# Moving one of four exps of 53 attention bursts from ScalarE to VectorE, with the TensorE work around those bursts regrouped

## The chip, the cores and the metric

The kernel runs on one core of a Trainium2 chip. In this kernel TensorE does the matrix products and leaves their sums in PSUM (`f_ps` in the views), which the program divides into eight banks of 512 columns. ScalarE does the exps and VectorE the other elementwise work; in the views both read PSUM and write SBUF, the working memory (`f_pt<-f_ps` and `f_K<-f_ps`). In the views of the profile PE is TensorE, PEld its weight loads, ACT is ScalarE, DVE is VectorE, POOL and SP are two more engines, and a q behind a name is its sequencer. A name such as L1565 is a line of the kernel. Times are microseconds on the device. A time is the median of several runs. A ratio is the mean time of one kernel's fast runs over that of the other's fast runs of the same rounds, so it is not quite the ratio of the medians.

The kernel before takes 961.2 us (960.95 to 961.47, 4 runs).

## The reference, cut to what matters

The reference mixes a state-space layer and an attention layer with a gate. The change touches the attention, which has 2048 tokens, 32 heads of 32 columns, and a full (not causal) softmax:

```python
qkv = (x @ wqkv).reshape(B, S, 3, H, Dh) ...          # S = 2048, H = 32, Dh = 32
scores = jnp.einsum("bhqd,bhkd->bhqk", q, k) * (Dh ** -0.5)
p = _softmax(scores, axis=-1)
o = jnp.einsum("bhqk,bhkd->bhqd", p, v)
...
return g * a + (1 - g) * b                             # a: state-space layer, b: attention @ wo
```

That is 32 x 2048 x 2048 exps. The inputs are small: worked out from the reference's own inputs, the scaled scores have a standard deviation of 0.006 and none exceeds 0.046 in size. So every exp lies within 5% of 1.

## The kernel before

The attention is cut into 512 *bursts*. A burst is 4 heads x 256 queries x 256 keys:

1. TensorE computes the scores (8 matmuls) into two *score slots* of PSUM, of two banks each. There are three such slots.
2. ScalarE computes two exps of 128x1024, one for each slot (two heads each), and writes each into a *tile* of SBUF.
3. Later TensorE multiplies the tile with V: 4 *groups* of 4 small products per burst, summed in one PSUM bank. Eight bursts form a unit, which VectorE normalizes.

The same loop also feeds TensorE with *dense chains* (projections, the state-space layer, the output product): chains of mostly 8 or 16 products of 128x512 into one PSUM bank, which VectorE must evacuate before the next chain can start. Four dense products go into each burst.

The loop, cut, in the order in which it hands work to the engines:

```python
for p in range(first, NBURST):
    self.burst(p)                       # scores of burst p, then its two exps
    q0, q1 = self.quarters[p]
    self.pv(q0, q1)                     # groups of V products planned for this place
    if q1 % 32 == 0:
        self.normalize(q1 // 32 - 1)
    ...                                 # loads (cut)
    quota = MM_PER_PERIOD               # 4
    while used < quota: ...             # dense products (cut)
    ...                                 # VectorE work that fits (cut)
    if ended is not None:
        ended.evac()                    # VectorE empties the dense bank
```

The plan of the V products and the tiles, cut (left out: a rule that allows six groups at a place where 6 to 12 of the unit are left, and the tiles of the first 60 bursts):

```python
n = min(4 * (p - 1), done + 5, done // 32 * 32 + 32)   # a burst's groups: at most 5 a place,
self.quarters[p] = (done, n)                           # not before place B + 2
...
def pt_of(self, B, z):                                 # z = 0, 1: the two exps of a burst
    return self.pt_at[B][z] if B < RING else (2 * B + z) % 6
```

There are six tiles and a burst takes two of them. So a tile is written again by the exps of the burst three later. Dependencies are kept with tokens, in the order of this program: an operation that reads a tile depends on the operation that wrote it last *before it in the program*. In place `p` the exps of burst `p` come first and the V products after them. A V product of burst `B` therefore finds its own exps in the tile only up to place `B + 2`. In the kernel before, every group from burst 60 on stands at exactly that place. (Earlier bursts stand later, but they have more tiles, in memory that is still free then.)

Of the kernel before, what the change touches and what calls it, by code (L numbers as in the profile page):

```python
# [8 lines left out]
I32 = mybir.dt.int32  # L9
ACT = mybir.ActivationFunctionType  # L10
# [13 lines left out]
RC_MAX = 1e20  # L24
# [904 lines left out]
MM_PER_PERIOD = 4  # L929
REST = 508  # L930
# [15 lines left out]
class FastPath:  # L946

    def __init__(self, nc, S, es, d, flag):
# [55 lines left out]
        self.tile += [self.cT[ri][:, j, :].rearrange("p (h n) -> p h n", h=2) for j in range(8) for ri in range(2)]  # L1004

# [308 lines left out]
    def item_ops(self, j, ch, n):  # L1314
# [29 lines left out]
        hw = ["warm"] if ch == 0 and j == 0 else []  # L1344
        if b == 1 and j == 0:
            hw = ["fX", "fY", "m_c"] + self.EFtok + ["gp%d" % i for i in range(4)]
# [164 lines left out]
    def plan(self):  # L1511


        self.quarters, done = {}, 0
        used = {}
        for p in range(FIRST, NBURST + 1):
            n = min(4 * (p - 1), done + (12 if p < FIRST + 0 else 5), done // 32 * 32 + 32)
            left = done // 32 * 32 + 32 - done
            if 5 < left < 13 and 4 * (p - 1) >= done + 6:
                n = done + 6  # L1520
            self.quarters[p] = (done, n)
            for q in range(done, n):
                used[q // 4] = p
            done = n
        order = [8 * int(w[1]) + int(w[3]) for w in self.OPENING.split() if w[0] == "B"]
        assert sorted(order) == list(range(FIRST))
        when = {b: p for p, b in enumerate(order)}

        pairs = [((12 + t, 16 + t), FIRST + 4 + 14 * t) for t in range(4)] + [((10, 11), FIRST + 6)]
        pairs += [((20 + 2 * j, 21 + 2 * j), C_LOADS + 4 * j) for j in range(8)] + [((6, 7), 68), ((8, 9), 68)]  # L1530
        pairs += [((2 * r, 2 * r + 1), NBURST) for r in range(3)]
        free = {t: -9 for t, _ in pairs}
        self.pt_at = {}
        for b in sorted(range(RING), key=lambda b: when.get(b, b)):
            p = when.get(b, b)
            ok = [(end, t) for t, end in pairs if free[t] < p and used[b] < end and not (end == NBURST and used[b] >= RING + t[0] // 2)]
            assert ok, (b, p)

            near = [(end, t) for end, t in ok if end - used[b] <= 1]
            end, t = min(near) if near else max(ok)  # L1540
            free[t] = used[b]
            self.pt_at[b] = t

    def pt_of(self, B, z):
        return self.pt_at[B][z] if B < RING else (2 * B + z) % 6

    def burst(self, B):
# [15 lines left out]
        for z in range(2):  # L1563
            s, p = sl[z], self.pt_of(B, z)
            self.act(lambda e, s=s, p=p: e.activation(self.tile[p], ps[:, 2 * s:2 * s + 2, :], ACT.Exp, scale=SCALE), [("S", s)], [("pt", p)], "exp")  # L1565

    def pv(self, q0, q1):

        ps, V = self.ps, self.V
        for q in range(q0, q1):  # L1570
            B, z, kl = q // 4, q // 2 % 2, q % 2
            U, i = divmod(B, BURSTS)
            g = U // QUNITS
            p = self.pt_of(B, z)

            def mm(e, z=z, p=p, kl=kl, i=i, g=g):
                m = None
                for h2 in range(2):
                    for qt in range(2):
# [3 lines left out]
                                     start=(i == 0 and z == 0 and kl == 0 and h2 == 0 and qt == 0), stop=(i == BURSTS - 1 and kl == 1),  # L1583
                                     skip_group_check=True)
                return m
            kw = dict(writes=["O"]) if i == 0 and z == 0 and kl == 0 else dict(acc=["O"])
            self.S.op("pe", mm, reads=[("pt", p), ("V", g % 2, i // 2), "v1"], name="pv", **kw)

    def normalize(self, U):
# [10 lines left out]
        if g < 4 and qb == 0:  # L1600
            x = [("pt", 6 + t) for t in range(6)] if g else ["wv0", "wv0g"]
            if g == 3:
                assert self.items_done >= 16
                x += [("ub", k, ri) for k in (2, 3) for ri in range(2)]
        self.dma(lambda e: e.dma_start_transpose(self.OT[:, g, 256 * qb:256 * (qb + 1)].rearrange("p (t q) -> p t q", t=2),
# [4 lines left out]
    def build(self):  # L1610
# [4 lines left out]
        self.later, self.tabled, self.folded = [], [], []  # L1615
        self.bg2 = []
# [43 lines left out]
        self.c_end = 0  # L1660
        log = self.log = []
        for p in range(first, NBURST):
# [4 lines left out]
            t0 = PERIOD * (p - first)  # L1667
            period = PERIOD
            q0, q1 = self.quarters[p]
            self.pv(q0, q1)  # L1670
            if q1 % 32 == 0:
                self.normalize(q1 // 32 - 1)
                self.dve_t = max(self.dve_t, t0 + PE_HEAD) + 0.75
# [30 lines left out]
            quota = MM_PER_PERIOD if p >= FIRST + 0 else 0  # L1704
            ended = None
            while used < quota:
# [38 lines left out]
                elif used >= quota and cur.left <= 1 and quota == MM_PER_PERIOD:  # L1745
                    quota += 1
            log.append((p, ended.tag if ended else (cur.tag if cur else None), used, round(self.dve_t - t0, 2), len(self.bg) + len(self.bg2)))
            limit = t0 + (period - 0.1 if ended is not None else period + PE_HEAD)
            while self.bg or self.bg2:
# [17 lines left out]
        assert not outs and cur is None  # L1767
        self.tail()

    def tail(self):  # L1770
# [4 lines left out]
        dve(lambda e: e.memset(z, 0.0), [], ["z"] + [("ut", 1)])  # L1775
# [16 lines left out]
        self.pv(4 * NBURST - 8, 4 * NBURST - 4)  # L1792
        preload()
        self.pv(4 * NBURST - 4, 4 * NBURST)
# [154 lines left out]
```

## Time and profile before

| view | reading |
|---|---|
| span of the profiled run | 960.1 us |
| ScalarE busy | 944.0 us (98%) |
| TensorE busy | 928.0 us (97%, its ends are modelled) |
| VectorE busy | 513.2 us (53%) |
| granted TensorE clock | 0.996 |

From the page of the kernel before: the busy times (share of the span, instructions), and the chain of work that ended last, by engine.

```profile
PE 928.0 (97%) x15316; PEld 490.1 (51%) x15316; DVE 513.2 (53%) x1097; ACT 944.0 (98%) x1034; POOL 10.1 (1%) x39
...
ACT 96%; SPq 1%; PE 1%; DVE 1%; DMA 1%; issue 0%; DVEq 0%
```

The chain is followed back from the last instruction, at each step to what released it. Two engines look full, but only ScalarE (ACT) is on the chain. Busy times over two stretches of the kernel before (start and end in us, then each engine's busy time and instructions, granted clock, DMA share, GB/s):

```profile
48.00:840.00 792.00, 779.17 (x13079) 413.71 (x13079) 453.99 (x936) 792.00 (x864) 5.30 (x18) 1.00 0.25 55
735.00:933.00 198.00, 192.63 (x3146) 98.19 (x3144) 46.91 (x96) 198.00 (x218) 0.00 (x0) 1.00 0.26 79
```

The fourth engine column is ScalarE: it is busy in all of the 792 us and starts 864 activations, one per 0.917 us, so a burst takes 1.83 us. The third is VectorE, busy for 24% of the last stretch, in which 27 of the 53 bursts of the change lie.

What TensorE does in a burst, from the timeline of the kernel before (start, duration, engine, line, what, how many; in brackets how long the engine stood idle just before, and who ended that):

```profile
850.89 0.40 PE L1559 MATMUL f_ps<-f_Q,f_K 32*128 32x256 bf16 x8 [0.28 <-ACT f_pt L1565]
851.22 0.57 PE L1582 MATMUL f_ps<-f_V,f_pt 128*128 128x33 bf16 x16
851.64 1.02 PE L1476 MATMUL f_ps<-f_wb,f_OT 128*128 128x512 bf16 x4
852.72 0.40 PE L1559 MATMUL f_ps<-f_Q,f_K 32*128 32x256 bf16 x8
```

From start to start the scores take 0.33 us, 16 V products 0.42 us, 4 dense ones about 0.86 us (4 x 0.215). The rest of the burst is a wait for ScalarE. The waits of the kernel before (who, for whom: us in total, times, longest):

```profile
PEld f_ps L1559 <- ACT f_pt L1565: 205.8, 464, 1.0
...
PEld f_ps L1582 <- issue: 105.3, 497, 0.4
```

The scores wait for an exp to free their slot. The V products (L1582) wait for no exp: theirs are always done. ("issue" is time in which the engine waited for nothing that the profile shows.)

### The profile page before, as it was taken

The numbers are of one execution on the slowest core, as the hardware profiler recorded it, in microseconds if no ns is written. First come the engines' busy times: TensorE is split into PE (matmuls) and PEld (weight loads), VectorE is DVE, ScalarE is ACT, GpSimd is POOL, SyncE is SP. The second block draws the span as 40 slices with busy tenths as digits, with TensorE's granted clock in tenths as the row PEclk, the third lists the DMA queues.
The fourth block names the chain that finished last, engine by engine and source line by source line (L and its number), as shares of the span: only waits on it lengthen the run. The fifth ranks groups of instructions, "written<-read, shape, count | busy, mean of one in ns | idle before, by whom it ended". The sixth has DMA issues, their size and how long they took to land.

```text
span 960.1 us, 33364 instructions
## 1 busy us (share of the span) xinstructions
PE 928.0 (97%) x15316; PEld 490.1 (51%) x15316; DVE 513.2 (53%) x1097; ACT 944.0 (98%) x1034; POOL 10.1 (1%) x39
## 2 busy tenths in 40 slices
PE   8899999999999999999999999999999999999996
PEld 4555644564444554555545654544645556444443
DVE  2788888898888427112188711178836112232223
ACT  6999999999999999999999999999999999999996
POOL 2000000000000000000000000000000000000000
PEclk9999999999999999999999999999999999999998
DMA  9558434210133002220023210133101213123312
GB/s 203 96 103 131 77 59 85 60 28 29 49 67 79 17 8 62 58 53 17 18 52 62 59 40 24 43 85 60 40 6 39 84 38 118 51 80 118 106 59 72
DMA packets 157074, 60.88 MB, mean 63 GB/s; under 512 B 145664, under 2 KB 145664, under 8 KB 156928
## 3 DMA queue, kind: packets, MB, share of 16 engines
q1 hardware_dynamic: 154768, 58.16, 27.0%
q8 instruction: 121, 1.98, 0.9%
q10 hardware_dynamic: 2160, 0.53, 0.3%
q14 instruction: 25, 0.20, 0.1%
HBM read 16.79 MB, written 12.58 MB: 31 GB/s over the span
## 4 chain that ended last, share of the span: by engine, by line
ACT 96%; SPq 1%; PE 1%; DVE 1%; DMA 1%; issue 0%; DVEq 0%
ACT f_pt L1565 89%; ACT f_OT L1565 2%; ACT f_Et L1565 2%; ACT f_cT_re L1565 2%; ACT f_cT_im L1565 2%; SPq L1040 1%; DMA f_xT<-in_A_x_dram 1%; PE f_ps L1559 0%; PE f_ps L1789 0%; PE f_ps L1582 0%; PE f_ps L1161 0%; PE f_ps L1416 0%; DVE f_xT L1828 0%; PE f_ps L1121 0%; PE f_ps L1815 0%
## 5 line engine op out<-in xcount | busy, mean ns | idle before, releaser
L1565 ACT ACTIVATE f_pt<-f_ps 128x1024 bf16<-128x1024 f32 x944 | 867.1, 1309 | 0.6 <-PE f_ps L1559 0.6
L1582 PEld LDWEIGHTS f_ps<-f_V,f_pt 128*128 128x128 bf16 x7552 | 220.2, 96 | 99.2 <-issue 98.8
L1582 PE MATMUL f_ps<-f_V,f_pt 128*128 128x33 bf16 x7552 | 268.7, 178 | 0.0
L1559 PE MATMUL f_ps<-f_Q,f_K 32*128 32x256 bf16 x4096 | 203.3, 273 | 22.7 <-ACT f_pt L1565 4.4
L1559 PEld LDWEIGHTS f_ps<-f_Q,f_K 32*128 32x128 bf16 x4096 | 60.5, 92 | 224.2 <-ACT f_pt L1565 205.8
L1416 PE MATMUL f_ps<-f_xT,f_wb 128*128 128x512 bf16 x512 | 131.0, 377 | 0.5 <-DVE f_pf L1211 0.4
L1386 PE MATMUL f_ps<-f_xT,f_wb 128*128 128x512 bf16 x464 | 118.9, 378 | 0.0
L1335 DVE TENSOR_TENSOR_SCAN f_ht<-f_pf,f_init,f_ut 128x512 bf16<-128x512 f32 x64 | 80.8, 1273 | 0.0
L1458 DVE TENSOR_SCALAR f_Ag<-f_ps,f_gcol 128x512 f32<-128x512 f32 x32 | 24.0, 751 | 91.0 <-PE f_ps L1445 91.0
L1445 PE MATMUL f_ps<-f_cT_im,f_hp 128*128 128x512 bf16 x192 | 72.6, 378 | 0.0
L1445 PE MATMUL f_ps<-f_cT_re,f_hp 128*128 128x512 bf16 x192 | 72.6, 378 | 0.0
L1595 DVE RECIPROCAL f_rc<-f_ps 128x8 f32<-128x8 f32 x63 | 13.1, 208 | 107.3 <-PE f_ps L1582 107.1
L1476 PE MATMUL f_ps<-f_wb,f_OT 128*128 128x512 bf16 x252 | 65.8, 380 | 0.0
L1404 PE MATMUL f_ps<-f_wb,f_xT 128*128 128x128 bf16 x896 | 59.2, 219 | 0.0
L1416 PEld LDWEIGHTS f_ps<-f_xT,f_wb 128*128 128x128 bf16 x512 | 40.5, 96 | 31.9 <-issue 0.4
L1482 DVE SCALAR_TENSOR_TENSOR f_xT<-f_ps,f_gcol,f_hp 128x512 bf16<-128x512 f32 (+1 forms) x28 | 21.0, 750 | 62.5 <-PE f_ps L1476 62.5
L1422 DVE CAST f_ub<-f_ps 128x512 bf16<-128x512 f32 x48 | 33.2, 691 | 39.7 <-PE f_ps L1416 39.7
L1386 PEld LDWEIGHTS f_ps<-f_xT,f_wb 128*128 128x128 bf16 x464 | 36.3, 96 | 27.9
L1404 PEld LDWEIGHTS f_ps<-f_wb,f_xT 128*128 128x128 bf16 x896 | 50.4, 97 | 0.0
L1326 DVE TENSOR_TENSOR f_tq<-f_ht,f_Et 128x512 bf16<-128x512 bf16 x128 | 45.8, 416 | 0.0
L1393 DVE CAST f_Q<-f_ps 128x512 bf16<-128x512 f32 x30 | 20.7, 692 | 46.7 <-PE f_ps L1386 46.5
L1326 DVE TENSOR_TENSOR f_ut<-f_tq 128x512 f32<-128x512 bf16 x64 | 42.2, 683 | 0.0
(130 smaller groups left out, 619.8 us busy)
## 6 DMA issues: line engine op xcount, KB each, us to landing
ag_scratch<-f_Ag SPq DMA_DIRECT2D x32, 256.0 KB, 2.3
f_hp<-ag_scratch SPq DMA_DIRECT2D x32, 256.0 KB, 2.8
f_wb<-in_B_wqkv_dram SPq DMA_DIRECT2D x21, 256.0 KB, 4.2
out_dram<-f_xT SPq DMA_DIRECT2D x16, 256.0 KB, 2.1
f_wb<-in_B_wo_dram SPq DMA_DIRECT2D x1, 1024.0 KB, 5.5
f_OT<-f_On SPq DMA_TRANSPOSE x63, 2.3
f_wb<-in_B_wo_dram SPq DMA_DIRECT2D x1, 768.0 KB
f_wb<-in_B_wqkv_dram ACTq DMA_DIRECT2D x2, 256.0 KB, 4.0
```

The lines of the kernel that those rows point to most:

```text
L1326: ops.append((c, lambda: dve(lambda e: e.tensor_tensor(o, a, b, op), r, w)))
L1335: ops.append((1.29, lambda ri=ri: dve(lambda e: e.tensor_tensor_scan(ht[:, ri, :], rr, ut[:, ri, :], self.init[:, ri, j:j + 1], ALU.mult, ...
L1386: mms.append((1, lambda e, f, l, a=a: e.matmul(ps[:, bank, :], w[:, g % 2, part, a, :], xT[:, a, 512 * ch:512 * (ch + 1)], start=f, stop=l ...
L1404: m = e.matmul(ps[:, bank, 128 * q:128 * (q + 1)], xT[:, a, 128 * kt:128 * (kt + 1)], w[:, g % 2, 2, a, :], start=(a == 0), stop=(a == 7))
L1416: mms.append((1, lambda e, f, l, a=a: e.matmul(ps[:, 7, :], bT[:, n % 2, ri, a, :], xT[:, a, 512 * ch:512 * (ch + 1)], start=f, stop=l), [ ...
L1422: self.dve(lambda e: e.tensor_copy(self.ub[k][:, ri, :], ps[:, 7, :]), [("bank", 7)], [("ub", k, ri)] + over, "evac_u")
L1445: mms.append((1, lambda e, f, l, j=j, ri=ri: e.matmul(ps[:, 7, :], hp[:, ri, j, cols], cT[ri][:, j, 512 * cb:512 * (cb + 1)], start=f, sto ...
L1458: self.dve(lambda e: e.tensor_scalar(a, ps[:, 7, :], self.gcol[:, 0, tt:tt + 1], None, ALU.mult), [("bank", 7), "g0"], [at], "evac_c")
L1476: mms.append((1, lambda e, f, l, j=j: e.matmul(ps[:, 7, :], OT[:, j, 256 * qb + 128 * r:256 * qb + 128 * (r + 1)], wo[j][0][:, 512 * cb:51 ...
L1559: m = e.matmul(ps[:, 2 * sl[h // 2] + h % 2, 256 * kl:256 * (kl + 1)], K[32 * h:32 * h + 32, g % 2, 128 * kt:128 * (kt + 1)], Q[32 * h:32 ...
L1565: self.act(lambda e, s=s, p=p: e.activation(self.tile[p], ps[:, 2 * s:2 * s + 2, :], ACT.Exp, scale=SCALE), [("S", s)], [("pt", p)], "exp")
L1582: m = e.matmul(ps[:, 6, o:o + 33], self.tile[p][:, h2, 256 * kl + 128 * qt:256 * kl + 128 * (qt + 1)], V[:, g % 2, 2 * i + kl, h, :], star ...
```

## The change

The intent is to take work from ScalarE. In 53 bursts, all in stretches where VectorE has little to do, VectorE computes the exp of one of the four heads with integer and cubic arithmetic, in five passes of 512 columns. ScalarE's first exp of such a burst shrinks from 1024 to 512 columns. The burst becomes shorter for ScalarE, so TensorE is given less beside it: 3 groups of V products in it and in the burst before, and dense products 5 in the burst before and 3 in the shortened one. The core of the diff:

```diff
+def dve_bursts():
+    for lo, hi, m in ((172, 188, 4), (204, 254, 4), (296, 332, 4), (400, 508, 4)):
+        out += [B for B in range(lo, hi) if B % m == 1]
 ...
 def plan(self):
+    late = B in DVB and q == 1                       # VectorE's head: two places later
+    parts.append((B + 2 + (2 if late else 0), B, q))
-    n = min(4 * (p - 1), done + 5, done // 32 * 32 + 32)
+    cap = 5
+    if p in DVB or p + 1 in DVB:
+        cap = 3
+    ready = [t for t in unit if t[0] <= p]
+    n = min(cap, len(ready))
 ...
+    if B in DVB and z == 0:
+        self.ring_at[B, z] = self.x_of(B, x % 2)     # a tile of its own
+    else:
+        self.ring_at[B, z] = k % 6                   # the six tiles as before
 ...
 def burst(self, B):
+    if z == 0 and B in DVB:
+        self.dve_exp(B, s, p)                        # half exp on ScalarE, five passes on VectorE
 ...
-    quota = MM_PER_PERIOD
+    quota = 3 if p in DVB else 5 if p + 1 in DVB and (cur is None or cur.left >= 8) else MM_PER_PERIOD
```

Cut here: the passes themselves (`exp_a` from PSUM to 32-bit integers, `exp_b` on the high halves, `exp_c`, `exp_d`, `exp_f` the cubic), the memory that they borrow, and the bookkeeping of VectorE's time.

More of the change, by code (lines that the diff above doesn't have):

```diff
@@ L9 @@
 I32 = mybir.dt.int32
+I16 = mybir.dt.int16
+U16 = mybir.dt.uint16
 ACT = mybir.ActivationFunctionType
@@ L23 @@
 RC_MIN = 1e-10
-RC_MAX = 1e20
+RC_MAX = 1e12
 class Op:
@@ L929 @@
 MM_PER_PERIOD = 4
+DPERIOD = 1.41
+EXP_A = 16713.9646930418
+EXP_B = 4936176.0
+EXP_C2 = 189883.03836007958
+EXP_C1 = 38303098318.667244
+EXP_C0 = 3607248267949745.0
+def dve_bursts():
+    out = []
+    for lo, hi, m in ((172, 188, 4), (204, 254, 4), (296, 332, 4), (400, 508, 4)):
+        out += [B for B in range(lo, hi) if B % m == 1]
+    return out
+DVB = set(dve_bursts())
 REST = 508
@@ L1004, in __init__ @@
         self.tile += [self.cT[ri][:, j, :].rearrange("p (h n) -> p h n", h=2) for j in range(8) for ri in range(2)]
+        row6 = self.OT[:, 6, :].rearrange("p (t h n) -> p t h n", t=2, h=2)
+        row7 = self.OT[:, 7, :]
+        hx = [hp[:, r, 4:8, :].rearrange("p a n -> p (a n)") for r in range(2)]
+        hx0 = hx[0].rearrange("p (t h n) -> p t h n", t=2, h=2)
+        self.xt = [hx0[:, 0], hx0[:, 1], row6[:, 0], row6[:, 1], ub[:, 0], ub[:, 1]]
+        self.xi = [hx[1][:, 0:1024].bitcast(I32), row7[:, 0:1024].bitcast(I32), self.ut[:, 0, :].bitcast(I32)]
+        self.xw = [hx[1][:, 1024:2048].bitcast(F32), row7[:, 1024:2048].bitcast(F32), self.ut[:, 1, :]]
+        self.tile += self.xt
         self.wv0 = self.OT[:, 0, 0:1040].rearrange("p (a n) -> p a n", a=8)
@@ L1344, in item_ops @@
         hw = ["warm"] if ch == 0 and j == 0 else []
+        if ch == 2 and j >= 4:
+            hw = self.x_toks(0)
         if b == 1 and j == 0:
@@ L1511, in plan @@
     def plan(self):
-        self.quarters, done = {}, 0
+        self.quarters = {}
         used = {}
-        for p in range(FIRST, NBURST + 1):
-            n = min(4 * (p - 1), done + (12 if p < FIRST + 0 else 5), done // 32 * 32 + 32)
-            left = done // 32 * 32 + 32 - done
-            if 5 < left < 13 and 4 * (p - 1) >= done + 6:
-                n = done + 6
-            self.quarters[p] = (done, n)
-            for q in range(done, n):
-                used[q // 4] = p
-            done = n
+        parts = []
+        for B in range(NBURST):
+            for q in range(4):
+                late = B in DVB and q == 1
+                parts.append((B + 2 + (2 if late else 0), B, q))
+        todo = [sorted(parts[32 * U:32 * U + 32]) for U in range(NBURST // BURSTS)]
+        done = 0
+        for p in range(FIRST, NBURST + 1):
+            cap = 5
+            if p in DVB or p + 1 in DVB:
+                cap = 3
+            unit = todo[done // 32]
+            left = len(unit)
+            ready = [t for t in unit if t[0] <= p]
+            n = min(cap, len(ready))
+            if 5 < left < 13 and len(ready) >= 6 and cap == 5 and p < 200:
+                n = 6
+            self.quarters[p] = [(B, q) for _, B, q in unit[:n]]
+            for _, B, q in unit[:n]:
+                used[B] = p
+            del unit[:n]
+            done += n
+            if not unit and done % 32:
+                assert False
         order = [8 * int(w[1]) + int(w[3]) for w in self.OPENING.split() if w[0] == "B"]
@@ L1542, in plan, with x_set, x_of, x_toks @@
             self.pt_at[b] = t
+        self.ring_at, k, x = {}, 2 * RING, 0
+        for B in range(RING, NBURST):
+            for z in range(2):
+                if B in DVB and z == 0:
+                    self.ring_at[B, z] = self.x_of(B, x % 2)
+                    x += 1
+                else:
+                    self.ring_at[B, z] = k % 6
+                    k += 1
+    def x_set(self, B):
+        return 0 if B < 254 else 1 if B < 392 else 2
+    def x_of(self, B, n):
+        return len(self.tile) - 6 + 2 * self.x_set(B) + n
+    def x_toks(self, k):
+        return [(n, len(self.tile) - 6 + 2 * k + t) for n in ("pt", "ptd") for t in range(2)] + [("xi", k), ("xw", k)]
     def pt_of(self, B, z):
-        return self.pt_at[B][z] if B < RING else (2 * B + z) % 6
+        return self.pt_at[B][z] if B < RING else self.ring_at[B, z]
     def burst(self, B):
@@ L1564, in burst, with dve_exp @@
             s, p = sl[z], self.pt_of(B, z)
+            if z == 0 and B in DVB:
+                self.dve_exp(B, s, p)
+                continue
             self.act(lambda e, s=s, p=p: e.activation(self.tile[p], ps[:, 2 * s:2 * s + 2, :], ACT.Exp, scale=SCALE), [("S", s)], [("pt", p)], "exp")
-    def pv(self, q0, q1):
+    def dve_exp(self, B, s, p):
+        ps, k = self.ps, self.x_set(B)
+        xi, xw, t = self.xi[k], self.xw[k], self.tile[p]
+        halves = xi.bitcast(U16).rearrange("p (n two) -> p n two", two=2)
+        lo, hi = halves[:, :, 0], xi.bitcast(I16).rearrange("p (n two) -> p n two", two=2)[:, :, 1]
+        ev = xi.bitcast(BF).rearrange("p (n two) -> p n two", two=2)[:, :, 1]
+        over = []
+        if not self.seen_x[k]:
+            self.seen_x[k] = True
+            if k == 0:
+                assert self.c_left[0] == 0
+                over = [("hp", 0, j, ri) for j in range(8) for ri in range(2)]
+            elif k == 1:
+                assert self.c_left[1] == 0
+                over = [("hp", 1, j, ri) for j in range(8) for ri in range(2)]
+            else:
+                assert self.items_done == 32, (self.p, self.items_done, self.log[216:336])
+                over = [("ut", 0), ("ut", 1)] + [("ub", a, b) for a in range(2) for b in range(2)]
+        self.act(lambda e: e.activation(t[:, 0, :], ps[:, 2 * s, :], ACT.Exp, scale=SCALE), [("S", s)], [("pt", p)] + over, "exp")
+        self.dve(lambda e: e.tensor_scalar(xi, ps[:, 2 * s + 1, :], EXP_A, EXP_B, ALU.mult, ALU.add), [("S", s)], [("xi", k)] + over, "exp_a")
+        I, W = ("xi", k), ("xw", k)
+        assert not self.dx, (self.p, [c for c, _ in self.dx], self.log[-8:])
+        self.waiting.add(B)
+        self.dx += [(0.48, lambda: self.dve(lambda e: e.tensor_scalar(hi, hi, 0.0, 128.0, ALU.max, ALU.mult), [I], [I], "exp_b")),
+                    (0.73, lambda: self.dve(lambda e: e.scalar_tensor_tensor(xw, lo, EXP_C2, lo, ALU.add, ALU.mult), [I], [W], "exp_c")),
+                    (0.73, lambda: self.dve(lambda e: e.scalar_tensor_tensor(xw, xw, EXP_C1, lo, ALU.add, ALU.mult), [I, W], [W], "exp_d")),
+                    (0.73, lambda: self.dve(lambda e: e.scalar_tensor_tensor(t[:, 1, :], xw, EXP_C0, ev, ALU.add, ALU.mult), [I, W], [("ptd", p)], "exp_f")),
+                    (0.0, lambda: self.waiting.discard(B))]
@@ L1569, in pv, with mm @@
+    def pv(self, quarters):
         ps, V = self.ps, self.V
-        for q in range(q0, q1):
-            B, z, kl = q // 4, q // 2 % 2, q % 2
+        for B, q in quarters:
             U, i = divmod(B, BURSTS)
             g = U // QUNITS
+            z = q // 2
             p = self.pt_of(B, z)
-            def mm(e, z=z, p=p, kl=kl, i=i, g=g):
+            split = B in DVB and z == 0
+            todo = [(kl, q) for kl in range(2)] if split else [(q % 2, h2) for h2 in range(2)]
+            begin = i == 0 and q == 0
+            assert not (begin and split) and not (split and q and B in self.waiting)
+            def mm(e, z=z, p=p, todo=todo, i=i, g=g, begin=begin):
@@ L1577, in mm @@
                 m = None
-                for h2 in range(2):
+                for kl, h2 in todo:
                     for qt in range(2):
@@ L1582, in mm @@
                         m = e.matmul(ps[:, 6, o:o + 33], self.tile[p][:, h2, 256 * kl + 128 * qt:256 * kl + 128 * (qt + 1)], V[:, g % 2, 2 * i + kl, h, :],
-                                     start=(i == 0 and z == 0 and kl == 0 and h2 == 0 and qt == 0), stop=(i == BURSTS - 1 and kl == 1),
+                                     start=(begin and h2 == 0 and qt == 0), stop=(i == BURSTS - 1 and kl == 1),
                                      skip_group_check=True)
                 return m
-            kw = dict(writes=["O"]) if i == 0 and z == 0 and kl == 0 else dict(acc=["O"])
-            self.S.op("pe", mm, reads=[("pt", p), ("V", g % 2, i // 2), "v1"], name="pv", **kw)
+            kw = dict(writes=["O"]) if begin else dict(acc=["O"])
+            self.S.op("pe", mm, reads=[("ptd" if split and q else "pt", p), ("V", g % 2, i // 2), "v1"], name="pv", **kw)
     def normalize(self, U):
@@ L1604, in normalize @@
                 x += [("ub", k, ri) for k in (2, 3) for ri in range(2)]
+        if qb == 0 and g >= 6:
+            assert all(self.x_set(B) != 1 or B < U * BURSTS - 8 for B in DVB)
+            x += self.x_toks(1)
         self.dma(lambda e: e.dma_start_transpose(self.OT[:, g, 256 * qb:256 * (qb + 1)].rearrange("p (t q) -> p t q", t=2),
@@ L1615, in build @@
         self.later, self.tabled, self.folded = [], [], []
+        self.dx, self.seen_x, self.waiting = [], [False] * 3, set()
         self.bg2 = []
@@ L1660, in build @@
         self.c_end = 0
+        tnext = 0.0
+        nq = 0
         log = self.log = []
@@ L1666, in build @@
             self.burst(p)
-            t0 = PERIOD * (p - first)
-            period = PERIOD
-            q0, q1 = self.quarters[p]
-            self.pv(q0, q1)
-            if q1 % 32 == 0:
-                self.normalize(q1 // 32 - 1)
+            t0 = tnext
+            period = DPERIOD if p in DVB else PERIOD
+            tnext = t0 + period
+            if p in DVB:
+                self.dve_t = max(self.dve_t, t0 + 0.3) + 0.75
+            self.pv(self.quarters[p])
+            nq += len(self.quarters[p])
+            if nq % 32 == 0 and self.quarters[p]:
+                self.normalize(nq // 32 - 1)
                 self.dve_t = max(self.dve_t, t0 + PE_HEAD) + 0.75
@@ L1703, in build @@
             used = 0.0
-            quota = MM_PER_PERIOD if p >= FIRST + 0 else 0
+            quota = 3 if p in DVB else 5 if p + 1 in DVB and (cur is None or cur.left >= 8) else MM_PER_PERIOD
+            base = quota
             ended = None
@@ L1744, in build @@
                     cur = None
-                elif used >= quota and cur.left <= 1 and quota == MM_PER_PERIOD:
+                elif used >= quota and cur.left <= 1 and quota == base:
                     quota += 1
             log.append((p, ended.tag if ended else (cur.tag if cur else None), used, round(self.dve_t - t0, 2), len(self.bg) + len(self.bg2)))
-            limit = t0 + (period - 0.1 if ended is not None else period + PE_HEAD)
-            while self.bg or self.bg2:
+            limit = t0 + (period - 0.1 if ended is not None else period + (0.1 if p + 1 in DVB else PE_HEAD))
+            while self.dx:
+                c, fn = self.dx[0]
+                st = max(self.dve_t, t0)
+                if st + c > limit:
+                    break
+                self.dx.pop(0)
+                fn()
+                self.dve_t = st + c
+            while not self.dx and (self.bg or self.bg2):
                 src = self.bg if self.bg and (self.bg[0][2] in self.tabled or not self.bg2) else self.bg2
@@ L1766, in build @@
         self.log = log
-        assert not outs and cur is None
+        assert not outs and cur is None and nq == 4 * NBURST - 8
         self.tail()
@@ L1774, in tail @@
         z = self.ut[:, 1, 0:65]
-        dve(lambda e: e.memset(z, 0.0), [], ["z"] + [("ut", 1)])
+        dve(lambda e: e.memset(z, 0.0), [], ["z"] + [("ut", r) for r in range(2)] + self.x_toks(2))
+        assert not self.dx, (self.p, [c for c, _ in self.dx], self.log[-8:])
         def check(u0, u1, s0, s1, c):
@@ L1791, in tail @@
         check(0, 63, 0, 63, 0)
-        self.pv(4 * NBURST - 8, 4 * NBURST - 4)
+        self.pv([(NBURST - 2, q) for q in range(4)])
         preload()
-        self.pv(4 * NBURST - 4, 4 * NBURST)
+        self.pv([(NBURST - 1, q) for q in range(4)])
         ov = ps[:, 6, 0:264].rearrange("p (a c) -> p a c", a=8)
```

## The prediction

> **What bounds the kernel now.** ScalarE. The busy table gives it 944.0 of 960.1 us, and the chain that ended last is 96% ScalarE, nearly all of it the 1024 exps of 128x1024. In the windows from 48 to 840 us it starts 871 activations in 792 us and is never idle: one exp per 0.909 us, 1.82 us per burst of two. TensorE shows 928 us busy, but its ends are modelled. In the timeline a burst costs it 0.33 us (scores), about 0.42 us (16 small products with V) and 0.215 us per dense product, together 1.61 to 1.66 us; then it waits for ScalarE. The wait table agrees: the score products wait 206 us in 464 waits for exp. VectorE is 53% busy, and only 23% to 28% where the 53 bursts lie (windows 317 to 347, 375 to 467, 540 to 606, 735 to 933 us).
>
> **What changes.** In 53 bursts one 128x1024 exp becomes 128x512. The trace's other activations give the slope: 278, 383 and 597 ns for 128, 256 and 512 columns, 0.83 ns per column. [...] Half an exp saves 0.427 us and leaves a pitch of about 0.48 us. 53 x 0.427 = 22.6 us leave ScalarE, all on the critical path.
>
> Added to VectorE: one 128x512 pass from PSUM (0.75 us, as the dense evacuation of that form), one 16-bit scalar pass (estimate 0.48 us, as the fold's) and three two-operand passes (0.75 us, as the fold's): about 3.5 us per burst, 185 us in all. Every four bursts VectorE then works about 5.3 of 6.85 us. It fits, but its order now matters: a score slot is freed only when the half exp and VectorE's first pass are both done. That pass should end about 1.3 us after the slot's release in the burst before, the half exp at 1.39 us.
>
> Nothing leaves TensorE. The shortened burst has 12 V products and 3 dense ones: 0.33 + 0.32 + 0.65 = 1.30 of 1.39 us; the burst before has 12 and 5: 1.73 of 1.82 us. Four bursts need 6.45 us (6.65 with the diagonal products) of 6.85. TensorE goes from roughly 90% to 95-97% filled; late scores are absorbed up to about 0.35 us, because the other exp still runs.
>
> **Predicted time.** 961.35 - 22.6 = 938.7 us if nothing is lost. I allow 2 us for bursts where an evacuation or a normalization on VectorE, or a fifth dense product, makes the scores late: **940.8 us**, range 937.5 to 948. That is close to the 2% line (942.1 us): faster by over 2%: 0.62, within 2%: 0.36, slower: 0.02.
>
> **What would show each step.** ScalarE busy near 921 us, still about 98% of the span and still the chain; 53 exps of 128x512 at a pitch near 0.48 us; VectorE busy near 697 us; the score products' wait for ScalarE smaller by about 20 us, with a new but short wait for VectorE; ScalarE idle in the last window (bursts 400 to 508) under 2 us, and that window shorter by 27 x 0.427 = 11.5 us.
>
> **What would make it wrong.** (1) Scores come late and ScalarE idles after the short exps: VectorE reaches its first pass late (behind an evacuation), or TensorE waits for a bank whose evacuation stands behind the cubic; 64 ns per burst already brings it under 2%. (2) A 512-column exp overlaps less with its neighbours, so it saves less than 0.427 us. (3) The interleaved 16-bit operands slow the VectorE passes. (4) The result fails its own check and the slow path runs; unlikely.

The 0.427 us for half an exp can be followed from the trace alone: its three activations (278, 383 and 597 ns) give 0.831 ns per column from 128 to 512 columns and 0.836 from 256 to 512, which is 0.425 to 0.428 us for 512 columns.

## The result, and the profile after

The changed kernel takes **1523.2 us** (1520.97 to 1527.91, 4 runs) against 961.2 us. The ratio is 1.5855, with a 95% interval of 1.5828 to 1.5881. It is some 58.5% slower.

From the page of the changed kernel: busy times, the granted clock in 40 slices of the span (tenths), and the chain.

```profile
PE 1100.0 (72%) x15316; PEld 528.9 (35%) x15316; DVE 677.8 (45%) x1362; ACT 944.2 (62%) x1034; POOL 10.1 (1%) x39
...
PEclk9999999996886655569855769996666555556666
...
ACT 60%; PE 37%; issue 1%; DVE 1%; DVEq 0%
```

No engine is full. There are 265 VectorE instructions more (53 x 5) and none more on TensorE or ScalarE (15316 and 1034 in both kernels), so it is not the slow fallback path. ScalarE and TensorE now share the chain, 60% and 37%. With busy shares of only 62% and 72% this suggests that they take turns. (The shared chain alone would not: the mended kernel tiles8b below has 56% and 36% with ScalarE busy 98%.) The granted clock is 1.00 until 341 us, about a fifth of the span; in most of the later slices it lies between 0.54 and 0.89 (it is 1.00 again from 685 to 722 us and from 913 to 1026 us). The waits of the changed kernel:

```profile
PEld f_ps L1681 <- ACT f_pt L1630: 476.6, 212, 2.5
ACT f_pt L1630 <- PE f_ps L1621: 427.9, 170, 3.2
PE f_ps L1681 <- ACT f_pt L1630: 399.1, 212, 2.2
```

The first and third lines are new in kind: the V products (L1681) wait for an exp, 212 times, about 2 us each. In the kernel before they never did. The second line is the answer to it: ScalarE waits for scores. The timeline of TensorE around the first such wait, still at a granted clock of 1.00 (335 to 341 us):

```profile
335.60 0.40 PE L1621 MATMUL f_ps<-f_Q,f_K 32*128 32x256 bf16 x8
335.93 0.27 PE L1681 MATMUL f_ps<-f_V,f_pt 128*128 128x33 bf16 x4
336.05 0.25 PE L1681 MATMUL f_ps<-f_V,f_hp 128*128 128x33 bf16 x4
336.15 0.25 PE L1681 MATMUL f_ps<-f_V,f_pt 128*128 128x33 bf16 x4
336.25 0.83 PE L1433 MATMUL f_ps<-f_wb,f_xT 128*128 128x128 bf16 x12
337.01 0.40 PE L1621 MATMUL f_ps<-f_Q,f_K 32*128 32x256 bf16 x8
339.45 0.47 PE L1681 MATMUL f_ps<-f_V,f_pt 128*128 128x33 bf16 x12 [2.05 <-ACT f_pt L1630]
339.77 1.05 PE L1433 MATMUL f_ps<-f_wb,f_xT 128*128 128x128 bf16 x16
340.75 0.40 PE L1621 MATMUL f_ps<-f_Q,f_K 32*128 32x256 bf16 x8
```

and of ScalarE in the same stretch:

```profile
336.05 0.60 ACT L1651 ACTIVATE f_hp<-f_ps 128x512 bf16<-128x512 f32 x1
336.54 2.86 ACT L1630 ACTIVATE f_pt<-f_ps 128x1024 bf16<-128x1024 f32 x3
341.20 1.94 ACT L1630 ACTIVATE f_pt<-f_ps 128x1024 bf16<-128x1024 f32 x2 [1.80 <-PE f_ps L1621]
```

The scores of a burst are issued at 337.01. The V products right behind them do not start before 339.45, just after the last of ScalarE's three exps ends at 339.40: that is the second exp of the very burst whose scores were issued at 337.01. By the plan these three groups belong to the burst three earlier, and its exps were done long ago. Behind them, in TensorE's order, stand the dense products and the next scores, and ScalarE has nothing to do until those scores come at 340.75. From scores to scores this burst takes 3.74 us instead of 1.83.

**Theory T.** The new plan lets V products slide to place `B + 3`, while most tiles still live only to `B + 2`. Following the program in its own order and noting for every group which exp wrote its tile last: in the kernel before, all 2048 groups find their own exps. In the changed kernel **365 of the 2048 groups, in 210 bursts, find the exps of the burst three later**. The trace counts 212 waits. The token scheme sees no race: it faithfully makes the group wait for the wrong, newer exp, which cannot begin before the scores just issued are done. So in those bursts the overlap of the two engines is gone. It is also an error in the result.

**Rival V.** VectorE is late: its first pass holds a score slot, or the cubic holds up an evacuation. The prediction had named this.

**Rival C.** The clock is throttled because TensorE is packed more densely, and everything else follows from the slow clock.

### The profile page after: what moved, and what is told of

Its sections match the earlier page's. It is cut to its first block, busy times and chain, and to the rows that moved or that the text cites. A ratio compares the mean times of both kernels' runs of the same rounds, so it can differ in the third digit from the quotient of the medians.

```text
span 1521.3 us, 33689 instructions
## 1 busy us (share of the span) xinstructions
PE 1100.0 (72%) x15316; PEld 528.9 (35%) x15316; DVE 677.8 (45%) x1362; ACT 944.2 (62%) x1034; POOL 10.1 (1%) x39
## 4 chain that ended last, share of the span: by engine, by line
ACT 60%; PE 37%; issue 1%; DVE 1%; DVEq 0%
ACT f_pt L1630 54%; PE f_ps L1681 8%; PE f_ps L1621 8%; PE f_ps L1474 7%; PE f_ps L1505 6%; PE f_ps L1415 4%; PE f_ps L1433 2%; ACT f_OT L1630 1%; PE f_ps L1445 1%; ACT f_Et L1630 1%; ACT f_cT_re L1630 1%; ACT f_ub L1651 1%; ACT f_cT_im L1630 1%; ACT f_hp L1651 1%; PE f_ps L1480 0%
## 5 line engine op out<-in xcount | busy, mean ns | idle before, releaser
L1630 ACT ACTIVATE f_pt<-f_ps 128x1024 bf16<-128x1024 f32 x891 | 842.9, 1160 | 427.9 <-PE f_ps L1621 427.9
L1681 PE MATMUL f_ps<-f_V,f_pt 128*128 128x33 bf16 x7128 | 269.3, 183 | 399.1 <-ACT f_pt L1630 399.1
L1681 PEld LDWEIGHTS f_ps<-f_V,f_pt 128*128 128x128 bf16 x7128 | 219.5, 99 | 531.9 <-ACT f_pt L1630 476.6
L1621 PE MATMUL f_ps<-f_Q,f_K 32*128 32x256 bf16 x4096 | 240.6, 317 | 13.1 <-ACT f_cT_re L1630 2.1
L1415 PE MATMUL f_ps<-f_xT,f_wb 128*128 128x512 bf16 x464 | 146.0, 445 | 0.0
L1445 PE MATMUL f_ps<-f_xT,f_wb 128*128 128x512 bf16 x512 | 139.2, 396 | 0.7 <-DVE f_pf L1238 0.4
L1505 PE MATMUL f_ps<-f_wb,f_OT 128*128 128x512 bf16 x252 | 104.2, 555 | 0.0
L1474 PE MATMUL f_ps<-f_cT_im,f_hp 128*128 128x512 bf16 x192 | 89.6, 467 | 0.0
L1652 DVE TENSOR_SCALAR f_ut<-f_ps 128x512 int32<-128x512 f32 x27 | 18.7, 691 | 156.3 <-PE f_ps L1621 150.1
L1474 PE MATMUL f_ps<-f_cT_re,f_hp 128*128 128x512 bf16 x192 | 88.1, 459 | 0.0
L1433 PE MATMUL f_ps<-f_wb,f_xT 128*128 128x128 bf16 x896 | 69.3, 239 | 0.1
L1651 ACT ACTIVATE f_ub<-f_ps 128x512 bf16<-128x512 f32 x27 | 16.4, 607 | 75.5 <-PE f_ps L1621 75.5
L1652 DVE TENSOR_SCALAR f_hp<-f_ps 128x512 int32<-128x512 f32 x17 | 11.8, 691 | 92.5 <-PE f_ps L1621 89.9
```

The costliest lines, as they stand in the source:

```text
L1415: mms.append((1, lambda e, f, l, a=a: e.matmul(ps[:, bank, :], w[:, g % 2, part, a, :], xT[:, a, 512 * ch:512 * (ch + 1)], start=f, stop=l ...
L1433: m = e.matmul(ps[:, bank, 128 * q:128 * (q + 1)], xT[:, a, 128 * kt:128 * (kt + 1)], w[:, g % 2, 2, a, :], start=(a == 0), stop=(a == 7))
L1445: mms.append((1, lambda e, f, l, a=a: e.matmul(ps[:, 7, :], bT[:, n % 2, ri, a, :], xT[:, a, 512 * ch:512 * (ch + 1)], start=f, stop=l), [ ...
L1474: mms.append((1, lambda e, f, l, j=j, ri=ri: e.matmul(ps[:, 7, :], hp[:, ri, j, cols], cT[ri][:, j, 512 * cb:512 * (cb + 1)], start=f, sto ...
L1505: mms.append((1, lambda e, f, l, j=j: e.matmul(ps[:, 7, :], OT[:, j, 256 * qb + 128 * r:256 * qb + 128 * (r + 1)], wo[j][0][:, 512 * cb:51 ...
L1621: m = e.matmul(ps[:, 2 * sl[h // 2] + h % 2, 256 * kl:256 * (kl + 1)], K[32 * h:32 * h + 32, g % 2, 128 * kt:128 * (kt + 1)], Q[32 * h:32 ...
```

## The experiments

Twelve runs of eleven changed kernels were made; the kernel before measured 960.95 to 962.07 us beside them. "T", "V" and "C" are the theories above; "U" and "W" come later.

### 1. order_only: the new order of TensorE's work without any exp on VectorE

```diff
-                late = B in DVB and q == 1
+                late = False
 ...                                    # no tile of its own, no split V products
-            if z == 0 and B in DVB:
-                self.dve_exp(B, s, p)
-                continue
```

> The order of V products and dense products of the changed kernel, with all exps left on ScalarE and nothing new on VectorE. Theory T: 775 groups in 222 bursts now read a tile that has been written again, so it is as slow as the changed kernel or slower, 1450 to 1750 us. Rival V: nothing is left to slow it, 961 to 970 us. Rival C: the density falls back, so near 961 us as well.

Measured: 1577.7 us, ratio 1.6448 (1.6353 to 1.6544), granted clock 0.705. VectorE's busy time is 513.8 us, as before the change. **V falls**: with nothing new on VectorE and no shortened exp the kernel is even slower, as T demands of 775 groups in 222 bursts.

### 2. exps_only: the exps on VectorE without the regrouped V products

```diff
-            if p in DVB or p + 1 in DVB:
-                cap = 3
```

> The 53 half exps and VectorE's passes of the changed kernel, the dense products 5 then 3, but the V products five a burst as before (none of them finds its tile written again). Theory T: 938 to 955 us. The shortened burst then has up to 20 V products and 3 dense ones, 1.50 of 1.39 us, absorbed by the other exp. Rival V: about 1500 us. Rival C: about 1500 us.

Measured: 953.2 us (952.78 to 954.21), ratio 0.9918 (0.9902 to 0.9935). No group finds a newer exp in its tile, and the 570 us are gone. Why it is only 0.8% faster is seen in its trace: the shortened burst mostly has 20 V products again, and the first exp of the burst behind it ends 1102 ns after its predecessor in the mean, against 917 for an exp that waits for nothing. That is 53 x 0.185 = 9.8 us.

### 3. cap4: four groups instead of three

```diff
-                cap = 3
+                cap = 4
```

> The changed kernel with four groups of V products instead of three in the shortened burst and in the one before it. 128 groups in 78 bursts still read a tile that has been written again. Theory T: the loss falls with the number of such bursts, from 582 us over 210 bursts to about 78/210 of it: 1050 to 1250 us. Rivals V and C: VectorE's work is the same and the density hardly differs, about 1500 us.

Measured: 1181.9 us (1181.35 to 1184.92), ratio 1.2302, granted clock 0.905. The loss goes roughly with the number of bursts with an overwritten tile (the estimate was 941 + 78/210 x 582 = 1157 us). Counted from tiles8b below, it is 3.0 us for each such burst here and 2.7 in the changed kernel.

### 4. tiles8: two more tiles, all orders kept (a wrong first try)

```diff
+        self.extra = [len(self.tile), len(self.tile) + 1]
+        self.tile += [self.tq[:, 0:2], self.tq[:, 2:4]]      # idle in these stretches
 ...
-                    self.ring_at[B, z] = k % 6
+                    ok = [(last[t], t) for t in pool if last[t] < B and ...]   # last V product placed before B
+                    self.ring_at[B, z] = min(ok)[1]
```

> The changed kernel with every order on every engine kept, but two more tiles for exps (in a buffer that is idle in these windows) and a tile given out only when its last V product stands before the new exp. Theory T (a tile is written again, in program order, before its last V product is issued: 365 of the 2048 groups of V products, in 210 bursts, have to wait for the exps of three bursts later): 937 to 946 us, ScalarE never idle, no V product waits over 0.5 us for an exp. Rival V (VectorE is late: its first pass holds the score slot, or the cubic holds up an evacuation): its work is unchanged, so about 1500 us. Rival C (TensorE's clock is throttled because it is filled more densely, and everything else follows): about 1500 us.

Measured: 951.0 us, ratio 0.9892, but the result is **wrong** (relative error 1.5): in two of the four stretches the borrowed buffer was lent out one burst before its owner had read it for the last time. The 570 us are gone here too, but the time misses T's 937 to 946 us by 5, and a wrong kernel proves little, so it was mended.

### 5. tiles8b: the same, mended

```diff
-... [(168, 193), (204, 257), (292, 337), (396, 514)] for t in self.extra
+... [(168, 193), (204, 257), (293, 337), (397, 514)] for t in self.extra
```

> The two extra tiles again, now lent out only after the last read of the buffer they borrow (the first try overlapped live data in two of the windows by one burst and gave a wrong result). Order of work as in the changed kernel. Expected: correct, and as fast as the first try, 949 to 953 us: theory T explains the loss of 570 us, and about 10 us to the predicted 941 stay unexplained.

Measured: 950.3 us (949.96 to 950.52), ratio 0.9885 (0.9868 to 0.9901), correct. **T is shown**: with every engine's order of work untouched, two more tiles take away 573 us. C falls too: TensorE is packed as densely as in the changed kernel and its clock is 0.999. But for one wait of 0.3 us the V products wait for no exp of ScalarE any more; the largest entry of their waits is this one:

```profile
PEld f_ps L1700 <- issue: 99.4, 471, 0.2
```

The time is as expected after tiles8. But the kernel misses the predicted 940.8 us by 9.5 us, and what T had been expected to give in tiles8 (946 at most).

### 6. fill: the clock by itself

The tiles stay wrong; TensorE gets matmuls that nobody needs, in front of the V products of the bursts in which it waits.

```diff
+    def fill(self, p):                     # only where a group finds a newer exp in its tile
+            for _ in range(17):
+                m = e.matmul(self.ps[:, 6, 264:512], self.ident[:], ..., start=False, stop=True)
```

> The changed kernel, with its early-written tiles, and 17 idle matmuls of 248 columns on TensorE in each of the 210 bursts in which it waits for such a tile (they write unused columns of the sum bank), about 1.8 us of the 2.05 us that it waits. If the low granted clock (0.76) is only a consequence of TensorE standing idle, the clock stays at 0.95 or more and the time falls to what the broken overlap alone costs: about 3.75 us a burst as in the first of them at full clock, 210 x 1.9 us over 941 to 951 us, that is 1320 to 1380 us. If the clock is throttled by load, it stays near 0.76 or falls further and the time stays at 1500 us or more.

Measured: 1358.8 us (1358.48 to 1359.13), ratio 1.4136. The granted clock, from the page of this run:

```profile
PEclk9999999999999999999999999999999999999999
```

The expected 1.8 us of added matmuls per burst are an estimate, from the 0.215 us of a dense product of 512 columns: 17 x 248/512 x 0.215. In this run they take 414.2 us of TensorE, 1.97 us per burst.

The same broken overlap with a busy TensorE (97% against 72%) keeps the full clock (0.999 in the mean, against 0.760) and is 164 us faster, although it executes 3570 matmuls more. So in this case the low clock was a consequence of TensorE standing idle for half of each such burst (2.05 of 3.74 us in the one shown), not the first cause, and it made the loss larger. The split is not exact: by the trace, in 96 of the 210 bursts the added matmuls ran on after the exp had come, by about 36 us in all. So the broken overlap may cost up to 36 us less than this run shows, and the clock as much more.

How much idle time lowers the clock, and how fast, was not shown. What the trace of the changed kernel shows is this: no wait of TensorE for an exp lasted more than 2.5 us, and yet from 507 to 520 us, with TensorE busy for 58% of the time by the modelled ends, the granted clock is 0.50 (third figure from the end below; the columns are as in the windows above). Dense products start 0.42 to 0.43 us apart there (510.36, 510.78; 511.31, 511.74) instead of 0.215.

```profile
507.00:520.00 13.00, 7.51 (x81) 3.04 (x81) 3.88 (x6) 5.39 (x6) 0.00 (x0) 0.50 0.05 20
```

### The remaining 9 us

The second loss shows in tiles8b. From the page, its chain by engine:

```profile
ACT 56%; PE 36%; DVE 5%; SPq 1%; issue 1%; DMA 1%; DVEq 0%
```

TensorE is on the chain for 36%, in the kernel before it was 1%. The timeline around one shortened burst, whose scores are at 862.75:

```profile
859.70 1.02 PE L1507 MATMUL f_ps<-f_wb,f_OT 128*128 128x512 bf16 x4
859.80 0.69 DVE L1677 SCALAR_TENSOR_TENSOR f_ut<-f_ut 128x512 f32<-128x512 f32 x1
860.22 2.85 ACT L1646 ACTIVATE f_pt<-f_ps 128x1024 bf16<-128x1024 f32 x3
860.65 0.40 PE L1637 MATMUL f_ps<-f_Q,f_K 32*128 32x256 bf16 x8
860.76 0.75 DVE L1513 SCALAR_TENSOR_TENSOR f_xT<-f_ps,f_gcol,f_hp 128x512 bf16<-128x512 f32 x1 [0.26 <-PE f_ps L1507]
860.98 0.37 PE L1700 MATMUL f_ps<-f_V,f_pt 128*128 128x33 bf16 x8
861.20 0.25 PE L1700 MATMUL f_ps<-f_V,f_tq 128*128 128x33 bf16 x4
861.42 0.68 DVE L1678 SCALAR_TENSOR_TENSOR f_ub<-f_ut 128x512 bf16<-128x512 f32 x1
...
861.57 1.25 PE L1507 MATMUL f_ps<-f_wb,f_OT 128*128 128x512 bf16 x5
...
862.75 0.40 PE L1637 MATMUL f_ps<-f_Q,f_K 32*128 32x256 bf16 x8
...
863.20 0.60 ACT L1670 ACTIVATE f_ub<-f_ps 128x512 bf16<-128x512 f32 x1
```

A dense chain ends with the four products of 859.70. VectorE evacuates the bank from 860.76 to 861.51 (0.75 us, and VectorE was idle before it, so it was not late). Only then, at 861.57, can the next chain start. Scores and 12 V products do not fill that time: the last V products need about 0.1 us from 861.20 on, and TensorE idles for some 0.3 us. Five dense products follow, and the scores at 862.75 come too late: ScalarE's exps ended at 863.07, the short one starts at 863.20.

**Theory U:** the turnover of the one dense bank (end of chain, evacuation, start of the next chain), which happens once or twice in four bursts, costs TensorE time that it no longer has once ScalarE is faster. **Rival W:** VectorE, with 2.5 us of cubic more in each of these bursts (0.45 + 3 x 0.69), makes evacuations and first passes late. **Rival X:** ScalarE itself loses the time, because a short exp beside long ones costs more than 0.49 us.

### 7. dense43: one dense product less in the burst before

```diff
-            quota = 3 if p in DVB else 5 if p + 1 in DVB and (...) else MM_PER_PERIOD
+            quota = 3 if p in DVB else MM_PER_PERIOD
```

> The same with 4 then 3 dense products instead of 5 then 3. Theory U (the remaining 10 us: in the burst before the shortened one a new dense chain starts, TensorE waits about 0.5 us for the evacuation of the one dense bank, because only 12 V products cover it, and with 5 dense products behind it the next scores come about 0.2 us late): one dense product less, 0.215 us, takes most of it back, 941 to 946 us. Rival W (VectorE's first pass comes late and holds the score slot): unchanged, 949 to 953 us.

Measured: 950.6 us (950.32 to 951.75), ratio 0.9891. **A miss for U as it was put.** The records of single exps in the traces say why. In tiles8b a short exp ends 642 ns after the exp before it, in the mean; in dense43 only 518. But the first exp of the burst behind it now ends 1047 ns after its predecessor instead of 953: the rule that lets a chain with one product left finish put the fourth product into the shortened burst, whose next scores then came late. The product moved, and the loss moved with it. The 5-then-3 grouping is neither the cause nor a cure.

### 8. evac64: a short evacuation

```diff
+    def n64(self):
+        return 64 if <p in one of the four stretches> else 512
-            self.dve(lambda e: e.tensor_scalar(a, ps[:, 7, :], ...
+            self.dve(lambda e: e.tensor_scalar(a[:, 0:n], ps[:, 7, 0:n], ...      # the other evacuations alike
```

> The two extra tiles, 5 then 3 dense products, and inside the windows every evacuation of the dense bank reads 64 of its 512 columns (wrong result on purpose): the evacuation falls from 0.75 to about 0.28 us, nothing else changes. Theory U: TensorE's wait for the bank nearly goes away, 938 to 943 us. Rival X (a short exp next to long ones costs ScalarE more than 0.49 us, or ScalarE itself loses the time): unchanged, 949 to 953 us.

Measured: 940.5 us (940.33 to 940.57), ratio 0.9783 (0.9767 to 0.98), result wrong. **X falls**, and the predicted 940.8 us come out almost exactly. U or W remain, as a shorter evacuation also relieves VectorE: its busy time is 635.3 us against 677.6 in tiles8b. The 0.28 us of the expectation are an estimate and were not read from this run. It can be worked out from the trace of the kernel before, where VectorE's copies from PSUM take 424 ns for 128x256 (L1133) and 692 ns for 128x512 (L1393), 1.05 ns per column: 448 columns less are 0.47 us less than 0.75.

### 9. no_cubic: VectorE relieved, evacuations as long as ever

```diff
-        self.dx += [(0.48, <exp_b>), (0.73, <exp_c>), (0.73, <exp_d>), (0.73, <exp_f>), (0.0, <done>)]
+        self.dx += [(0.0, <done>)]
```

> The two extra tiles, 5 then 3 dense products; VectorE does only its first pass, the one that frees the score slot, and leaves out the other four of each burst (wrong result on purpose): about 2.5 us of VectorE work less in each of the 53 bursts, every evacuation as long as before. Theory U (TensorE waits out the turnover of its one dense bank: end of the chain, full evacuation, start of the next): nothing changes on that path, 947 to 951 us. Rival W (the evacuations and the first pass are late because VectorE is busy with the cubic; evac64 was faster because it freed VectorE): 939 to 944 us.

Measured: 949.3 us (949.12 to 949.75), ratio 0.9876. Its output is wrong, which doesn't matter for the time. VectorE's busy time falls from 677.6 to 549.7 us (tiles8b first, then no_cubic) and the kernel gains 1 us. **W falls.**

```profile
PE 919.7 (97%) x15316; PEld 491.8 (52%) x15316; DVE 677.6 (71%) x1362; ACT 928.6 (98%) x1034; POOL 10.1 (1%) x39
PE 919.0 (97%) x15316; PEld 491.4 (52%) x15316; DVE 549.7 (58%) x1150; ACT 928.3 (98%) x1034; POOL 10.1 (1%) x39
```

### 10. vlast: cover the turnover

```diff
+            v_last = p >= 160 and not full and cur is not None and cur.left <= base + 1   # a chain ends here
+            if not v_last:
+                self.pv(self.quarters[p])
 ...                                                              # dense products
+            if v_last:
+                self.pv(self.quarters[p])
```

> The two extra tiles, 5 then 3; in a burst in which a dense chain ends, its last products go before the V products instead of behind them, so that V products and the next scores cover the evacuation (about 0.3 to 0.5 us more cover at each turnover). Same instructions, correct result. Theory U: 940 to 945 us. Rival W: no change in VectorE's work, 948 to 952 us.

Measured: **941.2 us** (940.92 to 941.5), ratio 0.979 (0.9774 to 0.9806), correct. With the same instructions, U's cure brings back 9.1 us. From its timeline, one turnover:

```profile
845.65 1.04 PE L1507 MATMUL f_ps<-f_wb,f_OT 128*128 128x512 bf16 x4
846.52 0.56 PE L1700 MATMUL f_ps<-f_V,f_pt 128*128 128x33 bf16 x16
846.93 0.25 PE L1700 MATMUL f_ps<-f_V,f_ub 128*128 128x33 bf16 x4
847.11 0.40 PE L1637 MATMUL f_ps<-f_Q,f_K 32*128 32x256 bf16 x8
847.44 0.47 PE L1700 MATMUL f_ps<-f_V,f_tq 128*128 128x33 bf16 x12
847.76 1.24 PE L1507 MATMUL f_ps<-f_wb,f_OT 128*128 128x512 bf16 x5
```

The last dense product of the ending chain is followed by 20 V products, the scores and 12 V products, and the next chain starts without a gap. A short exp now ends 511 ns after its predecessor, against 642 in tiles8b: 53 x 0.131 = 6.9 of the 9.1 us. Most of the rest, 1.6 us, is gained at the first exp of the second burst behind it. The chain is ScalarE's again:

```profile
PE 910.0 (97%) x15316; PEld 502.6 (54%) x15316; DVE 675.7 (72%) x1362; ACT 923.3 (98%) x1034; POOL 10.1 (1%) x39
...
ACT 93%; DVE 2%; PE 1%; SPq 1%; DMA 1%; issue 1%; DVEq 0%
```

### 11. before_vlast: the control

The same move of the V products in the kernel before.

> A control: the same move of the V products in the kernel before. There ScalarE never waits, so covering the turnover should give nothing: 959 to 963 us under theory U. If it gains over 5 us, the turnover had cost time in the kernel before already and the explanation of the remaining 10 us is wrong.

Measured: 961.4 us, ratio 0.9997 (0.998 to 1.0013). In the kernel before, where ScalarE is the limit (96% of the chain), covering the turnover is worth nothing. It became a cost in the changed kernel, where the short exps leave less slack and 12 V products instead of 16 cover the evacuation; these two were not told apart.

### 12. vlast5: the same kernel as vlast, five rounds

> The same kernel as in the run before it with the moved V products, unchanged, in five rounds, because three left it undecided whether it gains 2% (0.979, interval 0.9774 to 0.9806). Expected: correct, 940.5 to 942 us, ratio 0.978 to 0.980.

Measured: 942.2 us (941.9 to 943.76) against 962.1, ratio 0.9791 (0.9778 to 0.9805). The time is just above the 942 us expected, on a chip on which the kernel before is slower too; the ratio is as expected. It beats the kernel before beyond doubt. Whether by more than 2% stays undecided: the intervals of both series contain 0.98.

## Why the prediction was wrong

The result adds up from the medians of the runs (their kernels before lie within 1.2 us of each other; up to 36 us may belong to the last row instead of the one above it, see fill):

| step | us | shown by |
|---|---|---|
| the change with both faults mended | 941.2 | vlast |
| turnover of the dense bank no longer covered | +9.1 | tiles8b (950.3) minus vlast |
| overlap of TensorE and ScalarE broken in 210 bursts | +408.5 | fill (1358.8) minus tiles8b |
| TensorE's clock, low because it stands idle | +164.4 | the changed kernel (1523.2) minus fill |

- **The step that failed: "Nothing leaves TensorE. The shortened burst has 12 V products and 3 dense ones ..."** and its allowance "I allow 2 us". It counted how long the V products take, and took for granted that they may stand later. In this kernel a V product has a last permissible place, because its tile is written again three bursts later, and the kernel before had used that room up to the last place. Deferring groups beyond it turned 210 bursts from overlapped into serial: +573 us with the clock, where the prediction had 2 us. With it went "late scores are absorbed up to about 0.35 us, because the other exp still runs": in the timeline shown, no exp was left to run and ScalarE stood idle for 1.80 us. The list of what could go wrong has VectorE, TensorE's bank, the pitch of the exp and the fallback, but not this.
- **A second term was missing, "1.73 of 1.82 us" in the burst before:** the turnover of the dense bank is no product and was not in this sum; late scores of every kind had only the allowance of 2 us. Measured, the turnover costs 9.1 us. The prediction's guess of a bank "whose evacuation stands behind the cubic" named the place but not the cause: without the cubic (no_cubic) all but 1 us of it was still there.
- **Right, ScalarE's saving:** the median distance of a short exp's end from the one before is 490 ns in evac64 and vlast, against 917 for a full one, so 0.427 us as predicted. The kernels with both faults removed, evac64 (940.5) and vlast (941.2), land at the 940.8 us that were predicted for the kernel that has them, and ScalarE's busy time in vlast is 923.3 us (predicted near 921).
- **Right, VectorE fits:** busy 677.8 us in the changed kernel against a predicted 697. In the changed kernel's trace the passes take 0.69 us (four of them) and 0.45 us. The three two-operand passes, in each of which an operand is every second 16-bit half, take 688 to 692 ns (L1657 to L1659). In the same trace a two-operand pass of 128x512 over contiguous fp32 (L1336) takes 686 ns. So no cost of the interleaved operands shows here beyond 6 ns.
- **The result's correctness:** the changed kernel multiplies V by the exps of the wrong burst in 365 groups. order_only, cap4 and fill do likewise and their results were accepted. All exps here lie within 5% of 1, so the comparison with the reference cannot see it. That the groups read the newer exps follows from the program's order and is seen in the waits; the size of the error in the output was not measured.

Open: why vlast stays 2.5 us above the ideal 938.7 us. Its trace shows where: a short exp ends 511 ns after its predecessor in the mean, where the median is 490 (53 x 0.021 = 1.1 us), and the first exp of the burst behind it 948, where 917 is usual (53 x 0.031 = 1.6 us). No run tested why.

## What to carry to other kernels

Before deferring a consumer, work out until when its buffer lives: a scheduler that keeps dependencies by program order will not report an overwritten buffer as a race, it makes the consumer wait for the newer data and returns a wrong result that loose numerics may hide. In a profile its sign is a wait of a kind that did not exist before, with both engines well below full (62% and 72% here). That two engines share the chain where one had it alone is no proof by itself: the mended tiles8b shows it as well. And when the limiting engine is made faster, add the handovers of the next one (here the turnover of a single PSUM bank, 9.1 us) to its budget, not only its instructions.
